# Early attention scores as float16 pairs, and one unit's keys and values kept, in a fused attention and two-layer kernel on Trainium2

## The chip, the cores and the metric

The kernel runs on one core of one Trainium2 chip. The metric is the device time of one launch in microseconds (us), as the median of several runs. A profile is one further execution, recorded by the hardware profiler; its time is given beside the runs.

## The reference

```python
scores = (1 / sqrt(D)) * q @ k.transpose(0, 1, 3, 2)       # B=2, H=8, S=768, D=64, float32
keep = (key < n_sink) | ((row - key >= 0) & (row - key < window))   # n_sink 4, window 128
a = softmax(where(keep, scores, -1e9))                     # sum + 1e-9
x = (a @ v) as a matrix of 1536 x 512
h = x @ moe_w_in;  x = (h * tanh(softplus(h))) @ moe_w_out          # 512 -> 2048 -> 512
h = x @ moe2_w_in; x = (h * clip(h + 3, 0, 6) / 6) @ moe2_w_out     # 512 -> 2048 -> 512
```

The four weight matrices arrive as float64. The attention's inputs and the output are float32.

## The kernel before

**Precision.** The dense layers work on float16 pairs: a float32 number, scaled by a power of two, becomes a high half (rounded by ScalarE) and a low half (the remainder, by VectorE's `scalar_tensor_tensor`). A product of two such numbers is three TensorE products: high by high, high by low, low by high. Weights are decoded to such pairs on the chip, one *weight tile* at a time (`gen_decode`, L201: one VectorE operation of L208, two of L209 and L210, ScalarE's high half at L213, VectorE's low half at L216).

**Units.** The 1536 rows are cut into 12 units of 128 rows, 6 for each of the two batches. A row sees the 128 keys of its own unit, the 128 of the unit before it (not for the first unit of a batch), and up to 16 first keys of the batch, the *sinks*. `BLOCKS` (L1009) puts the units in three blocks of four, `[[6,7,0,1],[2,3,4,5],[8,9,10,11]]`, which pass through the dense layers one after the other.

**Early units** are those of the first two blocks, in that order: 6, 7, 0, 1, 2, 3, 4, 5. The class `First` handles them in float32, half a unit (4 of the 8 heads) at a time:

- `load_first` (L235): three loads of 256 KB for keys, queries and values.
- `prep` (L263): TensorE transposes keys and queries (L271), ScalarE copies them out of PSUM in float32 as `kt1` and `qt` (L272).
- `scores` (L284): for each pair of heads, one float32 product per head and block of keys (L296; the profile records a float32 product twice). VectorE adds the mask and takes the row minimum (L300), ScalarE takes the exponential (L304).
- `turn` (L309): TensorE transposes the exponentials (L315); the copies `at` out of PSUM are ScalarE's (L317) or, for the second block of keys in a unit's first half, VectorE's (L319). The 16 sinks go the same way (L323 to L326).
- `values` (L328): products with the values (L334 and L341). `normalise` (L344): division by the sums, `xf` (L350). `outputs` (L352): transposes (L356), and a high half by ScalarE (L359) and a low half by VectorE (L360) into the dense layers' input `xt`.

`first_blocks` (L364) interleaves these steps: each half's scores stand ahead of the other half's products, and a unit is prepared a unit ahead. Weight tiles of the first layer are decoded beside them.

**Late units** 8 to 11 run as generators beside the first dense layer: `hook()` (L783), called between groups of dense products, takes pieces of them at rates set at the end of the file (`RATES`, `AHEAD`). `gen_front` (L446) and `gen_keys` (L426) convert keys, values and queries to float16 pairs and transpose keys and queries by DMA (L434, L460). Their scores are float16 products (L480), with row minima (L487). The exponentials become float16 pairs `ag` and are transposed by DMA (L511); `gen_back` (L548) multiplies them with the values (L557, L558, L568). Unit 8 needs the keys and values of unit 7 and the sinks of its batch: all three are loaded a second time and converted again for the late units (L418 to L424, L451 to L455, L516 to L525).

```python
        if u - 1 not in last:                                 # gen_front, L451
            if b not in ks:
                yield from gen_sinks(b)
            yield from gen_keys(u - 1)
            load_unit(u)
        yield from gen_keys(u)
```

**Order.** The Tile scheduler places the instructions on each engine's queue from the order of the code and their dependences. SyncE (SP) issues nearly all DMAs, in order. `watch` (L101) is a VectorE check of a 64-column piece for numbers too small for float16 pairs; such input would go to `general_path` (L852), which is not taken here.

Of the kernel before, what the change touches and what calls it, by code (L numbers as in the profile page):

```python
# [16 lines left out]
BIG = 1.0e30  # L17
# [12 lines left out]
def attention_moe_moe2(  # L30
# [201 lines left out]
    kv_n = {}  # L232
    sink_n = {}

    def load_first(u, names="kqv"):  # L235
# [8 lines left out]
    def first_sinks(b):  # L244


        ks1 = c_p.tile([128, HP, 16], F32, name=f"ks1_{b}")
        nc.scalar.activation(out=ks1, in_=kv_n[b * NSB][0][:, :, 0:16], func=AF.Copy)
# [6 lines left out]
        sink_n[b] = (ks1, vsb)  # L255

    class First:
# [5 lines left out]
        def prep(self):  # L263
            u, b, i = self.u, self.b, self.i
            kn, qn, vn = (qkv_n[u][nm] for nm in "kqv")
            kt1 = v_p.tile([128, HP, 144], F32, tag="k", name="kt1")
            self.qt = v_p.tile([128, HP, 128], F32, tag="q", name="qt1")
            for dst, src, sc in ((kt1[:, :, 0:128], kn, 1.0), (self.qt, qn, -1.0)):
                tp = ps_acc.tile([128, HP, 128], F32, tag="acc", name="tp")
                for h in range(HP):  # L270
                    nc.tensor.transpose(tp[:, h, :], src[:, 2 * h:2 * h + 2, :].rearrange("p a d -> p (a d)"), ident)  # L271
                nc.scalar.activation(out=dst, in_=tp, func=AF.Copy, scale=sc)  # L272
            kv_n[u] = (kt1, vn)
            if i == 0 and b * NSB + 2 in first:
                first_sinks(b)
            if i > 0 and b * NSB + 2 in first:
                nc.gpsimd.tensor_copy(out=kt1[:, :, 128:144], in_=sink_n[b][0])
            self.kvs = {0: [u], 1: [u - 1, u]}.get(i, [u, u - 1])
            self.kvs = [kv_n[x] for x in self.kvs]
            self.n = 128 * len(self.kvs) + (16 if i > 1 else 0)  # L280
            self.mask = (m0, m1, m2)[min(i, 2)]

        def scores(self, g):
# [5 lines left out]
            for h0 in (4 * g, 4 * g + 2):  # L289

                sps = [ps_h.tile([128, n], F32, tag="h", name="s") for _ in range(2)]
                for m, kv in enumerate(self.kvs):
                    w_ = n - 128 if m else 128
                    for r in range(2):
                        rows = slice(64 * r, 64 * r + 64)
                        nc.tensor.matmul(sps[r][:, m * 128:m * 128 + w_], self.qt[rows, h0 // 2, :], kv[0][rows, h0 // 2, 0:w_], start=True, stop=True)  # L296
                for r in range(2):
                    h = h0 + r
                    hh = h % 4
                    nc.vector.tensor_tensor_reduce(  # L300
                        out=d[:, hh, 0:n], in0=sps[r], in1=self.mask, scale=SCALE, scalar=BIG,
                        op0=ALU.add, op1=ALU.min, accum_out=self.mins[:, h:h + 1],
                    )
# [24 lines left out]
        def values(self, g):  # L328
# [3 lines left out]
            if self.i > 1:  # L332
                vsb = sink_n[self.b][1][:, g].rearrange("p h d -> p (h d)")
                nc.tensor.matmul(self.o[:, 4 * g:4 * g + 4, :], self.ats[g], vsb, start=fresh, stop=False, skip_group_check=True)  # L334
                fresh = False
# [64 lines left out]

    kt = {}
    vt = {}
    ks = {}
    vs = {}
# [13 lines left out]
    def load_late(u):  # L418
        if u is None:
            return  # L420
        if u - 1 in last:
            load_unit(u)
        else:
            load_unit(u - 1, "kv")  # L424

    def gen_keys(u):  # L426
# [13 lines left out]
        nc.vector.scalar_tensor_tensor(out=v16[:, 1], in0=vn, scalar=2.0 ** SV, in1=v16[:, 0], op0=ALU.mult, op1=ALU.subtract)  # L440
        if u == last[0] - 1:
            watch(k16[:, 0, 0, :])
            watch(v16[:, 0, 0, :])
        yield

    def gen_front(u):  # L446
        b, i = divmod(u, NSB)
        at_p, at1_p = late["at"], late["at1"]
        if u - 1 not in last:
            if b not in ks:  # L450
                yield from gen_sinks(b)  # L451
            yield from gen_keys(u - 1)
            load_unit(u)
        yield from gen_keys(u)
# [5 lines left out]
        nc.sync.dma_start_transpose(out=qt, in_=q16.rearrange("p t h d -> p (t h d)"))  # L460
        if u == last[0]:
            watch(q16[:, 0, 0, :])
        load_late(next_late(u))
# [52 lines left out]
    def gen_sinks(b):  # L516

        at1_p = late["at1"]
        ksn = at1_p.tile([128, 512], F32, tag="xf", name="ksn")[0:16].rearrange("p (h d) -> p h d", h=H)
        nc.sync.dma_start(out=ksn, in_=k[b, :, 0:16, :].rearrange("h p d -> p h d"))  # L520
        k16 = at1_p.tile([128, 2, DM], F16, tag="x16", name="k16s")[0:16].rearrange("p t (h d) -> p t h d", h=H)
        nc.scalar.activation(out=k16[:, 0], in_=ksn, func=AF.Copy, scale=2.0 ** SK)
        nc.vector.scalar_tensor_tensor(out=k16[:, 1], in0=ksn, scalar=2.0 ** SK, in1=k16[:, 0], op0=ALU.mult, op1=ALU.subtract)
        ks[b] = at1_p.tile([128, 2 * HP, 16], F16, name=f"ks_{b}")
        nc.sync.dma_start_transpose(out=ks[b], in_=k16.rearrange("p t h d -> p (t h d)"))  # L525
        yield
        vsn = at1_p.tile([128, 512], F32, tag="xf", name="vsn")[:, 0:2 * D].rearrange("p (g d) -> p g d", g=2)
# [519 lines left out]
```

## Time and profile before

| | before |
|---|---|
| runs | 625.07, 626.54, 623.51 us; median 625.07 |
| profiled execution: time, span | 623.05 us, 621.3 us |
| TensorE (PE) | 600.8 us, 97% of the span, 3400 instructions |
| TensorE weight load (PEld) | 307.6 us, 50% |
| VectorE (DVE) | 376.0 us, 61%, 688 instructions |
| ScalarE (ACT) | 354.6 us, 57%, 640 instructions |
| GpSimd (POOL) | 14.2 us, 2% |
| DMA | 72.10 MB, 116 GB/s |

Busy times overlap, so they don't add up to the span. Weight loads run beside products and are listed apart. A float32 product counts as two instructions. The granted TensorE clock is at its upper level (9 tenths or more) in all 40 slices of the page. The execution lasts 1.75 us longer than its span.

### The profile page before, as it was taken

Reading aid. Unit: us, or ns where it says so; the run is one execution under the profiler, and the core shown is the slowest. Engines: PE = TensorE matmul, PEld = TensorE weight load, DVE = VectorE, ACT = ScalarE, POOL = GpSimd, SP = SyncE. Lnnn points to the kernel's source line nnn. Section 1 sums busy time; section 2 is a strip of 40 time slices with the busy share of each in tenths; the row PEclk is TensorE's granted clock in tenths of the full one; section 3 lists DMA queues with packets and bytes.
Section 4 is the critical chain, followed back from the end, with each engine's and each line's share of the span. In section 5 each row is a group of like instructions: output and inputs, shape, how many; then the busy total and the mean of one; then the engine's idle time right before and its main releaser. Section 6 shows DMA issues by size and latency. Waiting matters only on the chain.

```text
span 621.3 us, 8731 instructions
## 1 busy us (share of the span) xinstructions
PE 600.8 (97%) x3400; PEld 307.6 (50%) x3400; DVE 376.0 (61%) x688; ACT 354.6 (57%) x640; POOL 14.2 (2%) x28
## 2 busy tenths in 40 slices
PE   8999999899989999899999999999999999999995
PEld 5888865444444445444444444444444444444442
DVE  5678787889988554626988999844432322422221
ACT  5887676887788676647686765453343331413131
POOL 0010000600000000000000000000000000000000
PEclk9999999999999999999999999999999999999999
DMA  9865146897479313100344434598800100100002
GB/s 188 195 130 170 69 143 150 218 244 210 135 205 205 55 37 54 37 18 0 136 136 136 148 124 152 193 333 304 304 0 1 44 25 0 69 1 0 1 0 73
DMA packets 105832, 72.10 MB, mean 116 GB/s; under 512 B 73512, under 2 KB 98088, under 8 KB 105784
## 3 DMA queue, kind: packets, MB, share of 16 engines
q1 hardware_dynamic: 105784, 71.48, 41.3%
q8 instruction: 28, 0.46, 0.3%
q14 instruction: 20, 0.16, 0.1%
HBM read 60.43 MB, written 3.15 MB: 102 GB/s over the span
## 4 chain that ended last, share of the span: by engine, by line
PE 68%; DVE 14%; ACT 9%; DMA 4%; issue 3%; SPq 1%; ACTq 0%; DVEq 0%
PE acc L725 27%; PE h L666 9%; PE h L668 9%; PE h L667 9%; PE o L341 4%; PE s L296 3%; DVE g L690 2%; DVE e L683 2%; PE tp L315 2%; DVE p L209 2%; DVE p L210 2%; ACT w L213 1%; ACT e L678 1%; ACT e L679 1%; DVE w L216 1%
## 5 line engine op out<-in xcount | busy, mean ns | idle before, releaser
L666 PE MATMUL h<-xt,w 128*128 128x512 f16 x384 | 145.6, 379 | 1.3 <-DVE e L683 1.3
L667 PE MATMUL h<-xt,w 128*128 128x512 f16 x384 | 145.5, 379 | 0.0
L668 PE MATMUL h<-xt,w 128*128 128x512 f16 x384 | 145.5, 379 | 0.0
L725 PE MATMUL acc<-g,w 128*128 128x512 f16 x576 | 129.5, 379 | 2.7 <-DVE g L690 2.2
L725 PE MATMUL acc<-w,g 128*128 128x512 f16 x576 | 128.1, 379 | 0.0
L685 DVE SCALAR_TENSOR_TENSOR e<-e,h 128x512 f32<-128x512 f32 x48 | 32.8, 686 | 97.8 <-ACT e L672 97.8
L725 PEld LDWEIGHTS <-g 128*128 128x128 f16 x576 | 56.3, 98 | 68.0
L725 PEld LDWEIGHTS <-w 128*128 128x128 f16 x576 | 55.4, 98 | 69.0 <-issue 3.8
L672 ACT ACTIVATE e<-h,bias 128x512 f32<-128x512 f32 x48 | 32.7, 683 | 95.7 <-PE h L668 95.7
L690 DVE SCALAR_TENSOR_TENSOR g<-e,g 128x1024 f16<-128x1024 f32 x48 | 58.7, 1223 | 25.1 <-ACT g L689 24.9
L689 ACT ACTIVATE g<-e 128x1024 f16<-128x1024 f32 x48 | 50.6, 1055 | 31.7 <-DVE e L685 17.9
L668 PEld LDWEIGHTS <-w 128*128 128x128 f16 x384 | 37.6, 98 | 45.2
L667 PEld LDWEIGHTS <-w 128*128 128x128 f16 x384 | 37.6, 98 | 44.7 <-issue 1.3
L666 PEld LDWEIGHTS <-w 128*128 128x128 f16 x384 | 37.6, 98 | 44.6
L216 DVE SCALAR_TENSOR_TENSOR w<-p,w 128x1024 f16<-128x1024 f32 x32 | 39.1, 1222 | 14.5 <-ACT w L213 14.5
L213 ACT ACTIVATE w<-p 128x1024 f16<-128x1024 f32 x32 | 33.7, 1053 | 21.5 <-DVE p L210 21.1
L670 ACT ACTIVATE e<-h 128x512 f32<-128x512 f32 x48 | 28.3, 589 | 25.6 <-PE h L668 25.3
L186 ACT ACTIVATE y<-y 128x512 int32<-128x512 int32 x32 | 20.0, 625 | 37.0 <-DVE y L184 36.9
L683 DVE SCALAR_TENSOR_TENSOR e<-e,h 128x512 f32<-128x512 f32 x48 | 30.7, 681 | 16.9 <-ACT e L680 16.9
L209 DVE SCALAR_TENSOR_TENSOR p<-raw,p 128x1024 int32<-128x1024 int32 x32 | 39.1, 1223 | 0.7
L210 DVE SCALAR_TENSOR_TENSOR p<-raw,p 128x1024 int32<-128x1024 int32 x32 | 39.1, 1222 | 0.3
L304 ACT ACTIVATE d<-d,mins 128x272 f32<-128x272 f32 (+2 forms) x64 | 30.4, 479 | 6.6 <-DVE mins L300 6.6
(141 smaller groups left out, 582.6 us busy)
## 6 DMA issues: line engine op xcount, KB each, us to landing
raw<-in_moe_w_in_dram SPq DMA_DIRECT2D x48, 512.0 KB, 3.9
raw<-in_moe_w_out_dram SPq DMA_DIRECT2D x48, 512.0 KB, 5.1
first<-in_k_dram SPq DMA_DIRECT2D x8, 256.0 KB, 5.2
first<-in_q_dram SPq DMA_DIRECT2D x8, 256.0 KB, 5.0
first<-in_v_dram SPq DMA_DIRECT2D x8, 256.0 KB, 5.2
out_dram<-part SPq DMA_DIRECT2D x8, 256.0 KB, 2.2
nk<-in_k_dram SPq DMA_DIRECT2D x5, 256.0 KB, 3.2
nv<-in_v_dram SPq DMA_DIRECT2D x5, 256.0 KB, 4.2
```

The source lines that it names most:

```text
L209: nc.vector.scalar_tensor_tensor(out=p, in0=lo_w, scalar=29, in1=p, op0=ALU.logical_shift_right, op1=ALU.bitwise_or)
L210: nc.vector.scalar_tensor_tensor(out=p, in0=hi_w, scalar=-0x40000000, in1=p, op0=ALU.bitwise_and, op1=ALU.bitwise_or)
L213: nc.scalar.activation(out=w[:, :, 0, :], in_=pf, func=AF.Copy, scale=2.0 ** SW)
L216: nc.vector.scalar_tensor_tensor(out=w[:, :, 1, :], in0=pf, scalar=2.0 ** SW, in1=w[:, :, 0, :], op0=ALU.mult, op1=ALU.subtract)
L666: nc.tensor.matmul(o, wh, x[:, 0, c, :], start=c == 0, stop=False)
L667: nc.tensor.matmul(o, wh, x[:, 1, c, :], start=False, stop=False)
L668: nc.tensor.matmul(o, wl, x[:, 0, c, :], start=False, stop=c == KD - 1)
L683: nc.vector.scalar_tensor_tensor(out=e[:, i], in0=e[:, i], scalar=2.5, in1=hps[i], op0=ALU.subtract, op1=ALU.mult)
L685: nc.vector.scalar_tensor_tensor(out=e[:, i], in0=e[:, i], scalar=6.0, in1=hps[i], op0=ALU.min, op1=ALU.mult)
L689: nc.scalar.activation(out=gh, in_=e, func=AF.Copy, scale=sc)
L690: nc.vector.scalar_tensor_tensor(out=gl, in0=e, scalar=sc, in1=gh, op0=ALU.mult, op1=ALU.subtract)
L725: nc.tensor.matmul(o, l_, r_, start=first and m == 0 and x == 0, stop=last and end and x == 2, skip_group_check=True)
```

## The change

- The early units' keys and queries leave PSUM as float16 pairs: the high half by ScalarE, a new low half by VectorE, for keys and for queries of each unit. Their scores are three float16 products in place of one float32 product.
- The copies `at` in `turn` are all ScalarE's; six of them were VectorE's.
- Unit 7's transposed keys (`kt_front`) and its values as a float16 pair (`v_front`) stay in SBUF. The late units read these in place of a second load, conversion and transpose.
- The sinks' keys (`ks`) are copied by GpSimd from the transposed keys of a batch's first unit; their late load, conversion and transpose go.
- q, k and v of unit 8 are loaded at once (`load_late`), and the late stream's first unit is taken in 4 pieces ahead of its place, not 7; the others stay at 3.
- The checks `watch` sit on unit 6's `kt1` and `qt` and on unit 7's values.

```diff
     class First:
...
-            kt1 = v_p.tile([128, HP, 144], F32, tag="k", name="kt1")
-            self.qt = v_p.tile([128, HP, 128], F32, tag="q", name="qt1")
-            for dst, src, sc in ((kt1[:, :, 0:128], kn, 1.0), (self.qt, qn, -1.0)):
+            if u == last[0] - 1:
+                kt1 = const.tile([128, 2 * HP, 144], F16, name="kt_front")
+            else:
+                kt1 = v_p.tile([128, 2 * HP, 144], F16, tag="k", name="kt1")
+            self.qt = v_p.tile([128, 2 * HP, 128], F16, tag="q", name="qt1")
+            for dst, src, sc in ((kt1[:, :, 0:128], kn, 2.0 ** SK), (self.qt, qn, -(2.0 ** SQ))):
                 tp = ps_acc.tile([128, HP, 128], F32, tag="acc", name="tp")
...
-                nc.scalar.activation(out=dst, in_=tp, func=AF.Copy, scale=sc)
+                nc.scalar.activation(out=dst[:, 0:HP], in_=tp, func=AF.Copy, scale=sc)
+                nc.vector.scalar_tensor_tensor(out=dst[:, HP:2 * HP], in0=tp, scalar=sc, in1=dst[:, 0:HP], op0=ALU.mult, op1=ALU.subtract)
...
+            if u == last[0] - 1:
+                kt[u] = kt1
+                vt[u] = v16 = const.tile([128, 2, H, D], F16, name="v_front")
+                nc.scalar.activation(out=v16[:, 0], in_=vn, func=AF.Copy, scale=2.0 ** SV)
+                nc.vector.scalar_tensor_tensor(out=v16[:, 1], in0=vn, scalar=2.0 ** SV, in1=v16[:, 0], op0=ALU.mult, op1=ALU.subtract)
+                watch(v16[:, 0, 0, :])
+            if i == 0:
+                ks[b] = const.tile([128, 2 * HP, 16], F16, name=f"ks_{b}")
+                nc.gpsimd.tensor_copy(out=ks[b], in_=kt1[:, :, 0:16])
...
+                    for tq, tk in ((0, 0), (0, 1), (1, 0)):
+                        for r in range(2):
+                            rows = slice(64 * r, 64 * r + 64)
+                            nc.tensor.matmul(
+                                sps[r][:, m * 128:m * 128 + w_], self.qt[rows, tq * HP + h0 // 2, :], kv[0][rows, tk * HP + h0 // 2, 0:w_],
+                                start=tq + tk == 0, stop=tq == 1,
+                            )
...
-                if m <= g:
-                    nc.scalar.activation(out=at[:, m], in_=tp, func=AF.Copy)
-                else:
-                    nc.vector.tensor_copy(out=at[:, m], in_=tp)
+                nc.scalar.activation(out=at[:, m], in_=tp, func=AF.Copy)
...
     def gen_front(u):
...
-        if u - 1 not in last:
-            if b not in ks:
-                yield from gen_sinks(b)
-            yield from gen_keys(u - 1)
-            load_unit(u)
+        if b not in vs:
+            yield from gen_sinks(b)
         yield from gen_keys(u)
...
-        ahead = {u: 3 if u - 1 in last else 5 if u // NSB in {x // NSB for x in last[:n]} else 7 for n, u in enumerate(last)}
+        ahead = {u: 3 if u // NSB in {x // NSB for x in last[:n]} else 4 for n, u in enumerate(last)}
```

Three places show how the instructions move. The first is ScalarE at the start, where units 6 and 7 are prepared and unit 6's first exponentials follow. Before:

```order
L272 ACTIVATE kt_207<-tp 128x4x128
L272 ACTIVATE qt_208<-tp 128x512
L272 ACTIVATE kt_221<-tp 128x4x128
L272 ACTIVATE qt_222<-tp 128x512
L304 ACTIVATE d,sums<-d,mins 128x128 x8
L317 ACTIVATE at<-tp 128x512
```

and now:

```order
L277 ACTIVATE kt_207<-tp 128x4x128
L277 ACTIVATE qt_208<-tp 128x512
L277 ACTIVATE kt_front<-tp 128x4x128
L277 ACTIVATE qt_230<-tp 128x512
L287 ACTIVATE v_front<-first 128x512
L327 ACTIVATE d,sums<-d,mins 128x128 x8
L339 ACTIVATE at<-tp 128x512
```

The conversion of unit 7's values, which needs their load (`first`), stands ahead of the eight exponentials.

The second place is SP's queue where the late units' loads begin (`nk`, `nv`, `nq` are keys, values and queries of a late unit, `raw` halves of weight tiles, `ksn` and `vsn` the sinks). Before, from the second load on, the first being unit 7's `nk`:

```order
L411 DMA nv<-in_v_dram 128x8x64
L520 DMA ksn<-in_k_dram 16x8x64
L411 DMA nq<-in_q_dram 128x8x64
L434 DMA_TRANSPOSE kt_1397<-k_1394 128x8x128
L411 DMA nk<-in_k_dram 128x8x64
L525 DMA_TRANSPOSE ks_1336<-k16s 128x8x16
L530 DMA vsn<-in_v_dram 64x1x64 x4
L166 DMA raw<-in_moe_w_in_dram 128x4x256
L170 DMA raw<-in_moe_w_out_dram 128x1024
L411 DMA nv<-in_v_dram 128x8x64
L434 DMA_TRANSPOSE kt_1439<-k_1436 128x8x128
L460 DMA_TRANSPOSE qt<-q_1486 128x8x128
```

and now:

```order
L166 DMA raw<-in_moe_w_in_dram 128x4x256
L428 DMA nq<-in_q_dram 128x8x64
L428 DMA nk<-in_k_dram 128x8x64
L428 DMA nv<-in_v_dram 128x8x64
L527 DMA vsn<-in_v_dram 64x1x64 x4
L447 DMA_TRANSPOSE kt_1628<-k_1625 128x8x128
L170 DMA raw<-in_moe_w_out_dram 128x1024
L467 DMA_TRANSPOSE qt<-q_1673 128x8x128
```

The first key transpose and the sinks' transpose are gone, and the second half of a weight tile (L170) stands behind a key transpose that waits for unit 8's converted keys.

The third place is TensorE at the values of the last late unit, unit 11, which need the transposed weights `atg`. Before:

```order
L668 LDWEIGHTS w
L668 MATMUL h<-xt_89,w 128x512
L666 LDWEIGHTS w
L666 MATMUL h<-xt_89,w 128x512
L557 LDWEIGHTS atg
L557 MATMUL o<-vs_1_1368,atg 128x256
L558 LDWEIGHTS atg
L558 MATMUL o<-vs_1_1369,atg 128x256
```

and now:

```order
L722 LDWEIGHTS w
L722 MATMUL acc<-g_3098,w 128x512
L554 LDWEIGHTS atg
L554 MATMUL o<-vs_1_1594,atg 128x256
L555 LDWEIGHTS atg
L555 MATMUL o<-vs_1_1595,atg 128x256
```

Before, 55 products of the dense layer stand between this unit's last scores and its values; now 66.

## Rows read from the trace of the kernel before

**Rows 1.** Busy by stretch: us, PE, PEld, DVE, ACT, POOL (count), PEclk, DMA, GB/s

```profile
20.00:80.00 60.00, 59.71 (x517) 50.93 (x516) 47.19 (x161) 45.03 (x134) 2.75 (x6) 1.00 0.52 138
98.70:200.00 101.30, 96.38 (x583) 45.13 (x584) 90.23 (x146) 80.05 (x133) 10.05 (x12) 1.00 0.81 193
365.00:613.00 248.00, 248.00 (x1150) 112.40 (x1149) 102.50 (x128) 86.85 (x149) 0.00 (x0) 1.00 0.26 90
```

**Rows 2.** TensorE's waits, 100 to 275 us: total us, times, longest

```profile
PE s L480 <- DMA qt<-q: 1.8, 1, 1.8
PE s L480 <- DVE mins L487: 1.6, 2, 1.4
PE o L557 <- DMA atg<-ag: 1.6, 1, 1.6
PE h L666 <- DVE e L683: 1.3, 1, 1.3
```

**Rows 3.** Timeline of an early half unit: start us, us, instruction, [idle before <- releaser]

```profile
56.55 0.51 ACT L304 ACTIVATE d<-d,mins 128x272 f32<-128x272 f32 x1
...
57.47 1.05 PE L315 MATMUL tp<-ident,d 128*128 128x128 f32 x8
...
58.35 0.27 PE L325 MATMUL tp<-ident,ds 128*64 128x128 f32 x1
...
58.56 1.21 PE L296 MATMUL s<-kt,qt 64*128 64x128 f32 x16
...
59.70 0.66 PE L356 MATMUL tp<-ident,xf 128*128 128x128 f32 x4
```

**Rows 4.** The same view, TensorE at float16 scores of a late unit

```profile
119.34 0.53 PE L480 MATMUL s<-kt,qt 64*128 64x128 f16 x12 [1.80 <-DMA qt<-q]
119.80 0.39 PE L666 MATMUL h<-xt,w 128*128 128x512 f16 x1
```

**Rows 5.** VectorE's groups to 98.7 us: busy us, mean ns, idle before

```profile
L360 DVE TENSOR_TENSOR xt<-tp,xt 128x512 f16<-128x512 f32 x7 | 4.8, 687 | 0.7 <-ACT xt L359 0.7
...
L208 DVE TENSOR_SCALAR p<-raw 128x1024 int32<-128x1024 int32 x6 | 4.1, 690 | 0.0
L209 DVE SCALAR_TENSOR_TENSOR p<-raw,p 128x1024 int32<-128x1024 int32 x6 | 7.3, 1224 | 0.1
```

**Rows 6.** The same view from 98.7 to 275 us

```profile
L440 DVE SCALAR_TENSOR_TENSOR v<-nv,v 128x512 f16<-128x512 f32 x5 | 3.5, 703 | 0.1
```

**Rows 7.** Timeline of the start, SP's queue and ScalarE

```profile
4.98 2.33 SPq L241 DMA_DIRECT2D first<-in_v_dram  x2
...
10.47 0.40 ACT L304 ACTIVATE d<-d,mins 128x128 f32<-128x128 f32 x1 [0.15 <-DVE mins L300]
```

**Rows 8.** DMA issues: count, KB each, median us from issue to landing

```profile
first<-in_v_dram SPq DMA_DIRECT2D x8, 256.0 KB, 5.2
...
nk<-in_k_dram SPq DMA_DIRECT2D x5, 256.0 KB, 3.2
...
qt<-q SPq DMA_TRANSPOSE x4, 4.9
```

**Rows 9.** Timeline from the last early unit to the first late scores

```profile
98.01 0.69 DVE L350 TENSOR_TENSOR xf<-o,ri 128x512 f32<-128x512 f32 x1 [3.16 <-PE o L341]
...
112.28 3.63 SPq L434 DMA_TRANSPOSE kt<-k  x1
...
115.97 1.29 SPq L460 DMA_TRANSPOSE qt<-q  x1
```

**Rows 10.** Timeline of the last late unit, SP's queue and TensorE

```profile
248.47 0.53 PE L480 MATMUL s<-kt,qt 64*128 64x128 f16 x12
...
259.02 2.21 SPq L511 DMA_TRANSPOSE atg<-ag  x1
...
263.47 0.28 PE L557 MATMUL o<-vs,atg 128*128 128x256 f16 x1 [1.58 <-DMA atg<-ag]
```

**Rows 11.** Weight loads of late scores, 119 to 275 us, columns as in rows 5

```profile
L480 PEld LDWEIGHTS <-qt 64*128 64x128 f16 x192 | 5.9, 94 | 10.6 <-issue 10.6
```

More of the change, by code (lines that the diff above doesn't have):

```diff
@@ L233, in attention_moe_moe2 @@
     sink_n = {}
+    kt = {}
+    vt = {}
+    ks = {}
     def load_first(u, names="kqv"):
@@ L244, in first_sinks @@
     def first_sinks(b):
-        ks1 = c_p.tile([128, HP, 16], F32, name=f"ks1_{b}")
-        nc.scalar.activation(out=ks1, in_=kv_n[b * NSB][0][:, :, 0:16], func=AF.Copy)
         vsn = c_p.tile([64, 2, D], F32, name=f"vsn_{b}")
@@ L254, in first_sinks @@
             nc.gpsimd.tensor_scalar(out=vsb[:, :, h, :], in0=vsn, scalar1=selh[0:64, h:h + 1], scalar2=None, op0=ALU.mult)
-        sink_n[b] = (ks1, vsb)
+        sink_n[b] = vsb
     class First:
@@ L271, in prep @@
                     nc.tensor.transpose(tp[:, h, :], src[:, 2 * h:2 * h + 2, :].rearrange("p a d -> p (a d)"), ident)
-                nc.scalar.activation(out=dst, in_=tp, func=AF.Copy, scale=sc)
+                nc.scalar.activation(out=dst[:, 0:HP], in_=tp, func=AF.Copy, scale=sc)
+                nc.vector.scalar_tensor_tensor(out=dst[:, HP:2 * HP], in0=tp, scalar=sc, in1=dst[:, 0:HP], op0=ALU.mult, op1=ALU.subtract)
             kv_n[u] = (kt1, vn)
[L274 to L277, printed above, removed]
+            if u == first[0]:
+                watch(kt1[:, 0, 0:64])
+                watch(self.qt[:, 0, 0:64])
+            if u == last[0] - 1:
[7 more added lines that the diff above has]
+                nc.gpsimd.tensor_copy(out=ks[b], in_=kt1[:, :, 0:16])
+                if b * NSB + 2 in first:
+                    first_sinks(b)
+            else:
+                nc.gpsimd.tensor_copy(out=kt1[:, :, 128:144], in_=ks[b])
             self.kvs = {0: [u], 1: [u - 1, u]}.get(i, [u, u - 1])
@@ L293, in scores @@
                     w_ = n - 128 if m else 128
-                    for r in range(2):
-                        rows = slice(64 * r, 64 * r + 64)
-                        nc.tensor.matmul(sps[r][:, m * 128:m * 128 + w_], self.qt[rows, h0 // 2, :], kv[0][rows, h0 // 2, 0:w_], start=True, stop=True)
+                    for tq, tk in ((0, 0), (0, 1), (1, 0)):
[5 more added lines that the diff above has]
+                            )
                 for r in range(2):
@@ L300, in scores @@
                     nc.vector.tensor_tensor_reduce(
-                        out=d[:, hh, 0:n], in0=sps[r], in1=self.mask, scale=SCALE, scalar=BIG,
+                        out=d[:, hh, 0:n], in0=sps[r], in1=self.mask, scale=SCALE * 2.0 ** -(SQ + SK), scalar=BIG,
                         op0=ALU.add, op1=ALU.min, accum_out=self.mins[:, h:h + 1],
@@ L332, in values @@
             if self.i > 1:
-                vsb = sink_n[self.b][1][:, g].rearrange("p h d -> p (h d)")
+                vsb = sink_n[self.b][:, g].rearrange("p h d -> p (h d)")
                 nc.tensor.matmul(self.o[:, 4 * g:4 * g + 4, :], self.ats[g], vsb, start=fresh, stop=False, skip_group_check=True)
@@ L399, in open_late @@
         late["kv"] = main.enter_context(tc.tile_pool(name="kv", bufs=3))
-    kt = {}
-    vt = {}
-    ks = {}
     vs = {}
@@ L418, in load_late @@
     def load_late(u):
-        if u is None:
-            return
-        if u - 1 in last:
+        if u is not None:
             load_unit(u)
-        else:
-            load_unit(u - 1, "kv")
     def gen_keys(u):
@@ L440, in gen_keys @@
         nc.vector.scalar_tensor_tensor(out=v16[:, 1], in0=vn, scalar=2.0 ** SV, in1=v16[:, 0], op0=ALU.mult, op1=ALU.subtract)
-        if u == last[0] - 1:
-            watch(k16[:, 0, 0, :])
-            watch(v16[:, 0, 0, :])
         yield
@@ L460, in gen_front @@
         nc.sync.dma_start_transpose(out=qt, in_=q16.rearrange("p t h d -> p (t h d)"))
-        if u == last[0]:
-            watch(q16[:, 0, 0, :])
         load_late(next_late(u))
@@ L518, in gen_sinks @@
         at1_p = late["at1"]
[L519 to L526, printed above, removed]
         vsn = at1_p.tile([128, 512], F32, tag="xf", name="vsn")[:, 0:2 * D].rearrange("p (g d) -> p g d", g=2)
```

## The prediction

> **What bounds the kernel now.** I read the table by stretches first. From 365 to 613 us TensorE is busy for 248.0 of 248 us, all of it products of the two dense layers [rows 1]. The change touches none of these, so whatever it gains or loses must arise before 365 us. From 20 to 80 us, where seven of the eight early units run, TensorE is busy for 59.7 of 60 us, VectorE for 47.2 [rows 1]: TensorE sets the pace, and VectorE has about 2 us of 10 left. From 98.7 to 200 us the dense layer runs with the late units beside it; VectorE is busy for 90.2 of 101.3 us there [rows 1], and TensorE's waits come into view. The waits of TensorE between 100 and 275 us are four kinds, 6.3 us in all: 1.8 for the first transposed late query, 1.6 for the row minima of late scores, 1.6 for the last transposed weights of attention, 1.3 for VectorE's product that frees a score bank [rows 2].
>
> Within an early unit the timeline shows a loop of half units: the last exponential of a half starts at 56.55 and ends at 57.06, and the transposes of that half start at 57.47 [rows 3]. Between a half's scores and its transposes TensorE works on the other half and on the unit before. So the loop through VectorE and ScalarE is short of the bound by only 0.4 us: a faster TensorE soon meets it.
>
> **The change part by part.**
> *Scores of the early units.* Today the eight float32 products of a half unit (sixteen records) start at 58.56, and the next work starts at 59.70: 1.14 us [rows 3]. The new form is the late units': twelve float16 products (two heads, two blocks of keys) start at 119.34 and the next work at 119.80: 0.46 us [rows 4]. A half unit needs 24 of them. Twice 0.46 less one change of the array's shape is 0.83; that change costs 0.10, since transposes step 0.88/8 = 0.11 apart while the step from the last one to the scores is 0.21 [rows 3]. The gain is 0.31 us in each of 12 half units with two blocks of keys, 3.7 us, and I estimate half of that, 0.15, in the 4 with one block: **-4.3 us**. The order mixes scores and 128-row work more finely: TensorE changes shape 64 times up to the end of the early units, not 56: 8 x 0.10 = **+0.7**. Bounds for the two together: -4.3 and 0 (the loop above takes TensorE's place).
>
> [...]
>
> *Low halves.* Each early unit adds two VectorE operations of 128x512 out of PSUM, as the one that makes the low half of its output does today: 0.69 us [rows 5]; 16 x 0.69 = 11.0. Six copies of the same shape leave VectorE for ScalarE, at 0.69 each by the same row, and unit 7's values add 0.70 (as L440, [rows 6]). VectorE gets 7.6 us more before the early units end. The order also puts a seventh weight tile there, where six stand today: 0.69 + 3 x 1.22 = 4.4 us [rows 5]. If two thirds of these 12.0 fall between 20 and 80 us, VectorE goes from 47.2 to 55.2 of some 57, or 97%. Work in VectorE's queue then stands ahead of minima for which exponentials, transposes and TensorE wait. The trace shows no such load. From below the cost is 0 (it fills idle time); from above it is one more 0.69 in each of 14 half-unit loops, 9.7 us. I take **+1.0**, near the lower end: the low halves are made a unit ahead of their scores, and what is pulled forward of the weight tile can wait.
>
> *The start.* Unit 7's values are now converted early: the order puts this copy on ScalarE ahead of the first exponential. Two loads of values are issued from 4.98 to 7.31, the second from about 6.15 [rows 7]; with 5.2 us from issue to landing [rows 8] it lands at 11.3, and a copy of at most 0.7 ends at 12.0. The first exponential starts at 10.47 today [rows 7]. That moves ScalarE's exponentials by 1.5. VectorE's low half of the same tile (0.70, [rows 6]) and its check, which I take at 0.4 like the 128-column exponential [rows 7], stand between the second and third minima: they end at 13.1, the third minimum at 13.4, while the third exponential could start at 12.9 or so. TensorE has little else to do then. 1.5 and 0.4 make **+1.9**; bounds 0 (the load lands sooner) and 2.6 (all of it in a row).
>
> *First late scores.* Unit 7's keys stay in SBUF: one load, one conversion and one transposing DMA fall away from the chain, and q, k and v of unit 8 are loaded at once. Today that unit's query transpose is issued at 115.97, behind a key transpose that holds SP's queue for 3.63 [rows 9]. In the new order the scores stand 12 products of the dense layer earlier on TensorE, some 11.9 us after the last normalisation, which today starts at 98.01 [rows 9]. The loads start with that normalisation: 3.2 to 4 to land, 3 more until VectorE, which has four other operations first, has the keys' low half, 1.4 and 0.5 of issues on SP, then 4.9 for the transpose [rows 8]: 12.3 to 14 us. The wait of 1.8 becomes 0.4 to 2.1: **-0.7**, bounds -1.8 and +1.5. One half of a weight tile now queues behind the key transpose on SP; VectorE can wait up to 3 us for it, ahead of the first late minima.
>
> *Late VectorE work.* 0.70 + 0.70 of unit 7 [rows 6] and the tile done earlier, 4.4, leave the stretch that is 89% busy. I take half of the 2.9 us that TensorE waits there for VectorE (1.6 + 1.3): **-1.5**, bounds -2.9 and +3 (that half tile).
>
> *The last late unit.* Today its last scores start at 248.47, the transpose of its converted weights is issued at 259.02, and the product that needs them starts at 263.47 after 1.6 us of waiting [rows 10]: TensorE wants them 13.4 us after the scores. With three steps less to run in the late stream, the new order puts 66 dense products there, not 55, that is 11 x 0.216 (248.0/1150, [rows 1]) = 2.4 us more, less 0.5 of late work that moves too: **-1.5**, bounds -1.6 and 0. Nothing is late next: the products that read this unit's output come 54 dense products later in the new order.
>
> Loads, GpSimd copies and the dropped conversions of the first keys of the batch cost nothing in the sum: two loads of 256 KB fewer, on a stretch where GpSimd is nearly idle. If the queues are fuller than I think, they are part of the bounds above.
>
> Sum: -4.3 + 0.7 + 1.0 + 1.9 - 0.7 - 1.5 - 1.5 = -4.4 us on the profiled 623.05, or 618.65. The median of the three runs is 625.07, 2.02 above; on that scale I forecast **620.7 us**.
>
> **Rivals.**
> 1. *The half-unit loop sets the pace.* TensorE gains nothing from faster scores, since transposes wait for exponentials. For: only 0.4 us lie between the last exponential's end and the transposes. Against: TensorE has no idle time there that shows such a wait now. The -4.3 falls away: -0.1, or 625.0.
> 2. *VectorE becomes the bound of the early units, and the kernel is slower.* For: 97% by the count above, and one queue for minima, low halves and weight tiles. Against: low halves are wanted late. Price: 9.7 in place of 1.0, and no gain of 4.3: +8.6, or 633.7. It decides once VectorE's idle time between 20 and 80 us falls from 13 us to about 2.
> 3. *Everything falls into place.* No cost on VectorE (-1.0), all of the 2.9 us (-1.4), all of the query wait (-1.1): -7.9, or 617.2, and 614.6 if the start is hidden (-1.9) and the added shape changes cost nothing (-0.7); I round the range's end down to 614.
> 4. *Float16 weight loads don't overlap.* 336 loads of 94 ns [rows 11] are 31.6 us against today's 12 x 1.14 and half as much for the other 4, 16.0: +15.6 in place of -4.3, or 640.6. Against: 192 such loads are busy for only 5.9 us together, which the products overlap. [...]
>
> That the change might not do what it says is excluded by the order: late scores read the kept keys, and late products the kept values.
>
> **How the numbers follow.** A change under 0.5%, 3.1 us, cannot be told from none: faster is below 621.9, slower above 628.2. My forecast gets 0.50, with a range of its own from 617.5 to 624; it lies 1.2 below the border, so I count 0.39 of it faster and 0.11 the same. Rival 3 gets 0.13 (faster), rival 1 0.23 (same), rival 2 0.11 and rival 4 0.03 (both slower). Faster 0.52, same 0.34, slower 0.14. From 614 to 628 all but the two slower rivals is held, with the bounds of the start and the query wait.
>
> **What would show it.** Right: groups of 24 float16 products in about 0.8 us; the first early exponential at about 12 us; the last normalisation of the early units 1 us earlier than 98.0 to level with it; the wait for the transposed weights near 261 us gone; the stretch from 365 us on unchanged. Wrong: VectorE above 95% from 20 to 80 us with TensorE waiting for minima (rival 2), transposes that wait for exponentials in every half unit (rival 1), a first exponential still near 10.5, or a new wait over 2 us at the first late scores.

## The result and the profile after

The changed kernel takes 627.31 us (median of 20 runs, 625.53 to 636.15) against 624.5 (median of 20, 623.31 to 627.5): ratio 1.0062, interval 1.0044 to 1.0081. It is slower by 0.6%, where 620.7 was forecast. The ratios here and below, and the clocks in the table of runs, leave out runs more than 1.5% above the fastest of their kernel: one of the changed kernel (636.15 us), one of e14 (904.57 us) and four of the kernel before. The profiled execution of the changed kernel took 632.77 us, one of its longer ones: its mean clock is 0.979, and 15 of the 20 runs had 0.985 or more. So its length is not compared with the median.

The page of the changed kernel, its first lines and the row of the granted clock (40 slices of the span):

```profile
span 631.0 us, 8957 instructions
...
PE 606.9 (96%) x3512; PEld 310.3 (49%) x3512; DVE 381.1 (60%) x696; ACT 358.1 (57%) x643; POOL 14.8 (2%) x30
...
PEclk9599998999999999999999999999999999999999
```

The second slice reads 5 and the seventh 8, where the kernel before has 9 in all slices. The table by stretches of the changed kernel shows it closer (columns as in [rows 1]):

```profile
10.00:13.00 3.00, 1.18 (x13) 0.66 (x9) 2.46 (x14) 1.68 (x6) 0.00 (x0) 1.00 1.34 218
13.00:34.00 21.00, 21.00 (x144) 17.54 (x143) 12.25 (x51) 13.34 (x46) 1.06 (x4) 0.52 0.70 172
38.00:98.00 60.00, 59.26 (x586) 46.16 (x585) 53.15 (x155) 48.23 (x127) 3.44 (x6) 1.00 0.51 135
105.00:110.00 5.00, 4.22 (x16) 2.10 (x16) 4.93 (x7) 1.73 (x4) 1.26 (x2) 0.66 0.90 233
365.00:613.00 248.00, 247.28 (x1147) 111.99 (x1146) 109.23 (x135) 91.94 (x152) 0.00 (x0) 1.00 0.28 98
```

The same stretches of the kernel before:

```profile
10.00:13.00 3.00, 2.84 (x24) 2.11 (x24) 1.81 (x16) 2.85 (x14) 0.00 (x0) 1.00 1.33 218
13.00:34.00 21.00, 20.78 (x184) 17.73 (x183) 14.00 (x59) 17.48 (x59) 1.71 (x5) 1.00 0.86 206
```

From 10 to 13 us TensorE is now busy for 1.18 us, not 2.84. Then its granted clock is 0.52 for 21 us, that is, at its lower level (0.50 in every whole microsecond from 14 to 34 us) nearly throughout; it is back at 1.00 after 34 us. TensorE is busy for all of those 21 us and yet issues 144 instructions where 184 were issued. A second fall lies between 105 and 110 us. The stretch from 365 us on is nearly as before [rows 1].

The timeline of the changed kernel's start shows why TensorE has nothing to do:

```profile
10.34 0.68 DVE L278 SCALAR_TENSOR_TENSOR qt<-tp,qt 128x512 f16<-128x512 f32 x1
10.95 0.28 DVE L323 CUSTOM_DVE_ANT_0 d<-s,m 128x128 f32<-128x128 f32 x1
...
11.29 0.54 PE L316 MATMUL s<-kt,qt 64*128 64x128 f16 x6 [1.20 <-DVE mins L323]
11.32 0.63 ACT L287 ACTIVATE v_front<-first 128x512 f16<-128x512 f32 x1 [1.03 <-DMA first<-in_v_dram]
11.86 0.39 ACT L327 ACTIVATE d<-d,mins 128x128 f32<-128x128 f32 x1
11.98 0.69 DVE L288 SCALAR_TENSOR_TENSOR v_front<-first,v_front 128x512 f16<-128x512 f32 x1 [0.54 <-ACT v_front L287]
...
12.39 0.71 PE L338 MATMUL tp<-ident,d 128*128 128x128 f32 x2 [0.56 <-ACT d L327]
...
12.73 0.28 DVE L323 CUSTOM_DVE_ANT_0 d<-s,m 128x128 f32<-128x128 f32 x1
```

Low halves stand ahead of the first minimum (10.95), ScalarE waits for unit 7's values and converts them (11.32) ahead of the first exponential (11.86, [rows 7] have 10.47), and their low half stands ahead of the third minimum (12.73).

TensorE's waits between 100 and 275 us answer to [rows 2]; those of the dense layer and the late units are:

```profile
PE h L663 <- DVE e L680: 3.6, 2, 2.2
PE o L554 <- DMA atg<-ag: 1.7, 1, 1.7
PE s L485 <- DVE mins L492: 1.1, 1, 1.1
...
PE s L485 <- DVE e L680: 0.3, 1, 0.3
PE s L485 <- DMA qt<-q: 0.2, 1, 0.2
```

The wait for the query transpose nearly went (1.8 to 0.2), but that for VectorE's e (a tile of the dense layer's activation) grew from 1.3 to 3.6, and that for the last transposed weights stayed.

In the profiled executions, the first normalisation comes at 25.58 us (19.32 before), the last at 105.21 (98.01, [rows 9]), and the span ends 9.7 us later: 6.3 us are lost before the first, 0.9 between the two, 2.5 behind the last. The lower clock reaches over the first of these marks, to 34 us, so the 0.9 holds some of its cost too.

### The profile page after: what moved, and what is told of

Its sections match the earlier page's. It is cut to its first block, busy times and chain, and to the rows that moved or that the text cites. A ratio compares the mean times of both kernels' runs of the same rounds, so it can differ in the third digit from the quotient of the medians.

```text
span 631.0 us, 8957 instructions
## 1 busy us (share of the span) xinstructions
PE 606.9 (96%) x3512; PEld 310.3 (49%) x3512; DVE 381.1 (60%) x696; ACT 358.1 (57%) x643; POOL 14.8 (2%) x30
## 4 chain that ended last, share of the span: by engine, by line
PE 67%; DVE 15%; ACT 10%; issue 3%; DMA 2%; SPq 1%; ACTq 0%; DVEq 0%
PE acc L722 28%; PE h L663 9%; PE h L665 9%; PE h L664 9%; PE o L361 4%; DVE p L209 3%; DVE w L216 2%; DVE p L210 2%; PE tp L338 2%; PE s L316 2%; DVE g L687 2%; DVE p L208 2%; DVE e L680 2%; ACT w L213 2%; ACT e L675 1%
## 5 line engine op out<-in xcount | busy, mean ns | idle before, releaser
L722 PE MATMUL acc<-g,w 128*128 128x512 f16 x576 | 131.3, 382 | 2.5 <-DVE g L687 2.0
L216 DVE SCALAR_TENSOR_TENSOR w<-p,w 128x1024 f16<-128x1024 f32 x32 | 39.1, 1222 | 11.9 <-ACT w L213 11.9
L184 DVE TENSOR_SCALAR y<-raw 128x1024 int16<-128x1024 int16 x32 | 22.1, 689 | 19.5 <-DMA raw<-in_moe_w_out_dram 19.3
```

The lines of the kernel that those rows point to most:

```text
L216: nc.vector.scalar_tensor_tensor(out=w[:, :, 1, :], in0=pf, scalar=2.0 ** SW, in1=w[:, :, 0, :], op0=ALU.mult, op1=ALU.subtract)
L722: nc.tensor.matmul(o, l_, r_, start=first and m == 0 and x == 0, stop=last and end and x == 2, skip_group_check=True)
```

## The experiments

All medians are set against the kernel before in the same job (624.2 to 624.7); the clock is the mean granted clock of each run, lowest to highest. Where rows of two jobs are compared below, half a microsecond is within the doubt. "Pace" means three empty pieces in the late stream (e8).

The profiled execution of the kernel before, whose rows the prediction used, had a mean clock of 0.998. Of the 99 others that the ratios keep, 86 had 0.995 or less. So that profile, with the clock at its upper level in every slice, was one of the better executions.

| run | edit | median us | ratio (interval) | clock |
|---|---|---|---|---|
| after | the change | 627.31 | 1.0062 (1.0044 to 1.0081) | 0.975 to 0.992 |
| e1 | values later | 625.64 | 1.0022 (1.0005 to 1.0038) | 0.984 to 0.991 |
| e2 | start filler | 624.38 | 1.0009 (0.9992 to 1.0026) | 0.987 to 0.995 |
| e3 | before, stalled | 632.9 | 1.0128 (1.0106 to 1.015) | 0.981 to 0.991 |
| e4 | kept unit 7 alone | 629.87 | 1.0081 (1.0062 to 1.0099) | 0.991 to 0.995 |
| e5 | scores alone | 627.99 | 1.0055 (1.0037 to 1.0072) | 0.982 to 0.986 |
| e6 | copies back | 628.23 | 1.0085 (1.0056 to 1.0115) | 0.973 to 0.989 |
| e7 | values later, filler, copies back | 629.44 | 1.0087 (1.0064 to 1.011) | 0.983 to 0.988 |
| e8 | filler, pace | 622.74 | 0.9959 (0.9943 to 0.9975) | 0.990 to 0.997 |
| e9 | two fillers | 626.85 | 1.0022 (1.0006 to 1.0037) | 0.993 to 0.997 |
| e10 | two fillers, pace | 622.71 | 0.9973 (0.9956 to 0.999) | 0.990 to 0.997 |
| e11 | pace | 624.81 | 1.0025 (0.9996 to 1.0053) | 0.977 to 0.991 |
| e12 | values later, filler, pace | 620.21 | 0.9923 (0.9904 to 0.9943) | 0.994 to 0.996 |
| e13 | values later, pace | 620.84 | 0.9937 (0.992 to 0.9954) | 0.991 to 0.994 |
| e14 | kept unit 7, pace | 625.83 | 1.0025 (1.0008 to 1.0042) | 0.980 to 0.996 |

### The start and the clock: e1, e2, e3

e1 moves the four lines on `v_front` from `prep` into a method that is called behind unit 7's normalisation, with a write that orders them:

```diff
+            nc.vector.tensor_scalar(out=v16[:, 0, 0, 0:H], in0=self.sums, scalar1=0.0, scalar2=None, op0=ALU.mult)
             nc.scalar.activation(out=v16[:, 0], in_=vn, func=AF.Copy, scale=2.0 ** SV)
```

e2 adds to the change, in `first_blocks`:

```diff
         us[0].scores(0)
+        br = ps_acc.tile([128, 512], F32, tag="acc", name="br")
+        for _ in range(10):
+            nc.tensor.matmul(br, us[1].qt[:, 0, :], us[1].qt[:, 0:4, :].rearrange("p a n -> p (a n)"), start=True, stop=True)
         us[0].scores(1)
```

e3 adds to the kernel before the conversion of unit 7's values in `prep` (kept in `stall`), and in `scores`:

```diff
+            if self.u == first[0] and g == 0:
+                nc.vector.tensor_copy(out=d[:, :, 0:4], in_=stall[0][:, 0, 0, 0:16].rearrange("p (h s) -> p h s", h=4))
```

> The changed kernel, with the conversion of unit 7's values made to wait until unit 7's own row sums are known (a 128x8 VectorE write into the tile, from those sums, orders it); nothing else differs. Theory (the clock): the conversion at the start leaves TensorE with little work from 10 to 13 us, and the granted clock then falls to 0.50 from 13.2 to 34 us of the profiled run. Without it the first exponential starts at about 11.3, not 11.86, the mean clock returns to about 0.998, and the time to 620 to 621 us. Rival (VectorE): the low halves fill VectorE in the early units; moving one of them changes nothing, 626 to 628 us at a clock that stays near 0.99. Third possibility: the four low halves of units 6 and 7 alone, 2.7 us on VectorE, leave TensorE idle long enough; then the clock still falls, 624 to 627 us.

> The changed kernel, with ten more products of 128x512 float16 (2.2 us) between the first scores of unit 6, into a bank that nobody reads: they only keep TensorE at work from 10.3 us. All of VectorE's and ScalarE's work stands where the change put it. Theory (the clock): no fall of the granted clock after 13 us, 620 to 622 us in spite of added work. Rival (VectorE bound, or the late stream): the added products cost 0 to 2 us, 627 to 629 us.

> The kernel before, with unit 7's values converted at the start for nobody, and a 128x16 copy of them into the first exponentials' tile, so that unit 6's first row minima wait for the conversion; scores stay float32, no low halves. Theory (the clock): TensorE starves from about 10.5 to 12.5 us, the clock falls as in the changed kernel, and the time rises by the 2 us of the stall and 5 to 10 us of slow clock: 630 to 637 us, mean clock 0.975 to 0.99. Rival: the stall alone, 626 to 627 us at 0.998.

Stretches of e2, then of e1, then of e3:

```profile
10.00:13.00 3.00, 2.64 (x18) 0.96 (x18) 2.52 (x14) 1.72 (x6) 0.00 (x0) 1.00 1.35 218
13.00:34.00 21.00, 20.42 (x229) 17.13 (x228) 17.16 (x74) 19.27 (x67) 1.69 (x5) 1.00 0.83 203
```

```profile
10.00:13.00 3.00, 1.78 (x18) 1.01 (x13) 2.46 (x17) 1.99 (x10) 0.00 (x0) 0.71 1.32 216
13.00:34.00 21.00, 20.87 (x206) 17.47 (x206) 14.74 (x65) 17.16 (x60) 1.06 (x4) 0.88 0.75 187
```

```profile
10.00:13.00 3.00, 0.31 (x6) 0.12 (x4) 0.85 (x3) 0.93 (x2) 0.00 (x0) 0.82 1.36 217
13.00:34.00 21.00, 20.73 (x151) 18.38 (x152) 12.46 (x60) 16.18 (x59) 3.92 (x7) 0.78 0.71 174
```

With ten useless products in the gap (e2) TensorE is busy for 2.64 of the 3 us, the clock stays at 1.00, and the median is 2.9 us lower than the change's although work was added. With the values later (e1) TensorE still has a gap of 1.2 us ahead of the second half of the scores, and the clock still falls to 0.50, for a shorter time in this execution (11.2 to 18 us). And in the kernel before, a stall of that kind alone (e3; its longest wait is 3.0 us) brings the fall, to 0.50 from 12 to 22 us, and costs 8.7 us, with the stall itself and two more falls further on in it. So the fall of the clock behind a gap in TensorE's work is shown, in both kernels.

The profiles of all runs agree. The seven in which TensorE waits over 1 us for the first minima (3.0 us in e3, 1.2 in the change, e1, e5, e6, e11 and e13) have a clock of 0.50 somewhere between 10 and 20 us. The three without that wait (before, e4, e14; 0.2 us) and the six with fillers (e2, e7 to e10, e12) have 1.00 throughout there. How long such a fall lasts differs by execution: 21 us in the profile of the change, 6.8 us (12.6 to 19.4) in that of e11, whose start is the same.

The expected 620 to 621 us of e1 and 620 to 622 us of e2 didn't come: the clock was not all. The time of e1 lies in the range of its third possibility, that the low halves alone leave TensorE idle long enough.

### The halves, and what follows the early units: e4, e5, e6, e7, e9

e4 is the change with float32 scores, copies and sinks as before; behind unit 7's normalisation it converts the sinks' keys, unit 7's keys and its values:

```diff
+                nc.scalar.activation(out=hi, in_=src, func=AF.Copy, scale=sc)
+                nc.vector.scalar_tensor_tensor(out=lo, in0=src, scalar=sc, in1=hi, op0=ALU.mult, op1=ALU.subtract)
```

e5 is the kernel before with `prep`, `scores` and `first_sinks` of the change (no values converted, no `watch` in `prep`). e6 takes one line of the change back, and e7 is e1 with that and with eight fillers as in e2:

```diff
-                nc.scalar.activation(out=at[:, m], in_=tp, func=AF.Copy)
+                if m <= g:
+                    nc.scalar.activation(out=at[:, m], in_=tp, func=AF.Copy)
+                else:
+                    nc.vector.tensor_copy(out=at[:, m], in_=tp)
```

e9 adds to e2, in the last early unit:

```diff
+            if f is None:
...
+                for _ in range(NF):
+                    nc.tensor.matmul(br, xs[:, 0, :], xs, start=True, stop=True)
             e.values(1)
...
+NF = 6
```

> The kernel before with only the second half of the change: unit 7's keys and values and the sinks' keys are kept as float16 pairs for the late units (converted from the float32 tiles once unit 7's row sums are known), the late stream is shortened as in the change. Early scores stay float32, the copies stay where they were. Theory (only the start and the clock went wrong): the late terms of the prediction come, up to 3.7 us less three added operations, 621 to 623 us. Rival (the late terms are wrong: VectorE's and the transposes' waits only move): 624 to 626 us, and the waits of TensorE between 100 and 275 us still sum to 6 us or more.

> The kernel before with only the first half: early queries and keys as float16 pairs and their scores as float16 products; the late units load and convert unit 7 and the sinks as before, and the copies of transposed exponentials stay where they were. No values are converted at the start, but four low halves still stand ahead of the first minima. Theory (clock): the gap at the start is shorter (first minimum at about 10.7, not 12.7 for the third), so the clock falls for a shorter time or not at all; from the first output of unit 6 to the last normalisation 2.5 us less than before; 621 to 625 us with a clock of 0.988 to 0.995. Rival (VectorE bound): no gain between those two marks and waits of TensorE for minima, 625 to 628 us.

> The changed kernel with the six copies of transposed exponentials given back to VectorE, as before. Theory: the second fall of the clock (105.9 to 109 us in the changed kernel's profile, 97.8 to 100.9 with the filler) follows waits of TensorE for these copies on ScalarE (0.7 us) ahead of the last outputs; with them gone it does not fall there, 1.5 to 2 us less: 625 to 626 us, the start unchanged. Rival (it follows the wait for the last normalisation, which stays): 627 to 628 us.

> The changed kernel with three mends at once: unit 7's values converted later, eight filler products among unit 6's first scores, the six copies back on VectorE. Theory (clock): no fall of the clock before 200 us, mean clock 0.995 to 0.998, 621 to 622.5 us, faster than both kernels. Rival (the late stage takes back what the early units gain): 623.5 to 625 us at that clock.

> The kernel of e2 with six more filler products (1.3 us) ahead of the last early unit's second half of values, where TensorE waits for sinks' weights and for copies on ScalarE (0.4 and 0.7 us at 93 to 95.5). Theory (clock): the fall of the clock at 97.8 to 100.9 us goes, 1 to 2 us less than e2, 622.5 to 623.5 us, at a mean clock near 0.998. Rival (the fall follows the wait for the last normalisation, or comes at random): it stays, 624 to 625 us.

Each half alone is slower than before. In e5 the clock falls twice: it is 0.71 from 10 to 13 us and 0.88 from 13 to 34, and 0.57 from 95 to 107, where the last early unit waits 2.1 us for a copy on ScalarE. From its first to its last normalisation (22.50 to 100.75) it gains 0.4 us, not the expected 2.5. Its time lies in its rival's range, but not for the rival's reason: TensorE waits 0.2 us for minima between those marks. e4 was a miss on both sides (621 to 623 us expected, 624 to 626 by its rival). Its larger waits between 100 and 275 us sum to 8.7 us, as its rival had it (6 or more):

```profile
PE h L669 <- DVE e L686: 3.6, 2, 2.2
PE s L491 <- DMA qt<-q: 2.2, 1, 2.2
PE o L560 <- DMA atg<-ag: 1.8, 1, 1.8
PE s L491 <- DVE mins L498: 1.1, 1, 1.1
```

e6 and e7 were misses. In e6, with the copies back, the last early unit waits for a copy on ScalarE longer (2.1 us, 0.7 in the change), and the clock is at its lower level from 96.5 to 106.8 us. In e7 that wait is 0.7 again, but the clock is at its lower level from 97.7 to 104.5 us, and between 100 and 275 us TensorE waits 5.8 us for VectorE's e, more than in any other run. e9 (622.5 to 623.5 us expected) came out above its rival's range too. It moved a fall and did not remove it: the one at 97.8 us is gone, one at 112.6 us follows a wait of 2.0 us for the first late query. Filling single gaps by hand there led nowhere.

### The pace of the late stream: e8, e10, e11, e12, e13, e14

e8 adds these lines to e2; they make e10 of e9, e11 of the change, e13 of e1 and e14 of e4, and e12 is e13 with five fillers:

```diff
         if b not in vs:
+            for _ in range(3):
+                yield
             yield from gen_sinks(b)
...
-        ahead = {u: 3 if u // NSB in {x // NSB for x in last[:n]} else 4 for n, u in enumerate(last)}
+        ahead = {u: 3 if u // NSB in {x // NSB for x in last[:n]} else 7 for n, u in enumerate(last)}
```

> The kernel of e2 (change and start filler) with three empty pieces ahead of the late stream's first unit, and 7 in place of 4 taken ahead: the pieces that the change removed are counted again, so that late attention work stands at about the same places of the dense layer as before. Theory (pace): with three pieces fewer the late work comes earlier, bunches with weight decoding, and TensorE waits 3.6 us for VectorE's e where it waited 1.3; with the pieces back the waits between 100 and 275 us fall from 8.8 us (e2) to 5 to 6.5, and the time to 620.5 to 622.5 us. Rival (the late terms were never there): waits only move, 623.5 to 625 us.

> Both together: the three empty pieces and both fillers. Theory: 619 to 621.5 us, faster than both kernels, with a mean clock of 0.996 to 0.998. Rival (neither pace nor the second fall decides): 623 to 625 us.

> The changed kernel with only the three empty pieces (and 7 taken ahead), no filler at the start. Theory (two separate causes): the start's slow clock stays (0.50 for 7 to 21 us from about 12 us on), the late stage is as in e8; against the change, the late pace gives back about 1.6 us (e8 against e2), 625 to 627 us at a mean clock of 0.985 to 0.99. Rival (the pace is nearly all of it): 622 to 624 us.

> The kernel of e8 with unit 7's values converted later as well (as in e1) and five fillers at the start, not ten. Theory: the third minimum no longer stands behind a conversion, so the first output of unit 6 comes 1 us sooner than in e8 (20.0, not 20.96) and the clock holds at the start; if the late stage keeps e8's order, 621.5 to 622.5 us. Rival (the order of the late stage comes out otherwise, as in e7): 623.5 us or more, with new waits of TensorE between 95 and 200 us.

> The kernel of e12 without its five filler products: unit 7's values later and the three empty pieces. Theory (the clock at the start is a cause of its own): low halves and checks still stand ahead of the first minima, TensorE is short of work from 10 to 11.3 us, the clock falls near 11.5 us as in e1 (6.6 us at half there), and the time is 2 to 4 us above e12: 622 to 624 us at 0.988 to 0.991. Rival (with the third minimum free the filler does nothing): 620 to 621 us at 0.994 or more.

> The kernel of e4 (float32 scores, unit 7 kept) with the three empty pieces. Theory (pace): of e4's 5.2 us over the kernel before, the part behind the last normalisation (4.5 us) goes: 624.5 to 626.5 us, and its waits between 100 and 275 us fall from 9 us to 5 to 6.5. Rival (keeping unit 7 is itself what costs there): 628 us or more.

The empty pieces take no time of any engine; they only let `hook()` count what the change had removed. Each kernel gains by them: 1.6 us (e2 to e8), 2.5 (the change to e11), 4.1 (e9 to e10), 4.8 (e1 to e13), 4.0 (e4 to e14), by the medians. The profiles show where: from the last normalisation of the early units to the end of the span, the seven kernels that keep unit 7 without the pieces (the change, e1, e2, e4, e6, e7, e9) take 525.2 to 529.4 us, the six with them 520.9 to 524.2, and the kernel before 523.3. Four forecasts of times were off all the same: e8 and e10 came out above theirs, e12 below, e11 between its range and its rival's.

The waits of e8 between 100 and 275 us:

```profile
PE o L559 <- DMA atg<-ag: 1.6, 1, 1.6
PE h L668 <- DVE e L685: 1.4, 1, 1.4
PE acc L727 <- DVE g L692: 0.7, 1, 0.7
PE s L490 <- DVE mins L497: 0.4, 1, 0.4
PE h L668 <- DVE mins L497: 0.2, 1, 0.2
```

They sum to 4.3 us, against 7.8 in e2 (not 8.8, as the expectation has it), and those for e are at 1.4 again. What the pieces pull apart stands in the changed kernel's timeline just ahead of 200 us:

```profile
196.62 1.04 ACT L512 ACTIVATE ag<-d 128x1024 f16<-128x1024 f32 x1
...
197.56 1.04 ACT L677 ACTIVATE e<-e 128x1024 f32<-128x1024 f32 x1
197.69 1.23 DVE L515 SCALAR_TENSOR_TENSOR ag<-d,ag 128x1024 f16<-128x1024 f32 x1 [1.57 <-ACT ag L512]
...
198.83 1.28 DVE L680 SCALAR_TENSOR_TENSOR e<-e,h 128x512 f32<-128x512 f32 x2
199.57 0.38 PE L663 MATMUL h<-xt,w 128*128 128x512 f16 x1 [2.22 <-DVE e L680]
```

A conversion of a late unit's weights stands ahead of the dense layer's activation on both engines (1.04 us on ScalarE, 1.23 on VectorE), and TensorE waits 2.2 us for the bank. With the pieces back, the order turns: in e8 VectorE's e comes at 201.35 us and the low half of the weights behind it at 202.56.

e13 and e12 are faster than both kernels. Their difference, 0.6 us, lies within their intervals: with the values out of the way the filler decides nothing that these runs can tell, although the clock of e13 still falls behind its gap (0.92 from 13 to 34 us, a fall of 3.4 us). So e13 missed its forecast of 2 to 4 us above e12; the rival's time came, with a clock lower than the rival had. e13 against the change removes no work and adds one 128x8 operation: 627.31 to 620.84. The two edits are worth more together (6.5 us) than one by one (1.7 in e1, 2.5 in e11); why was not settled. e14 came as expected and stays 1.3 us above the kernel before, so keeping unit 7 alone gains nothing even at the old pace. The likely reason, not tested by itself, is that its conversions from float32 tiles are added work in the early units: the last normalisation came 2.4 us later in e4 (100.42 against 98.01).

## Why the prediction was wrong

**The start failed, in its price.** The step said "TensorE has little else to do then", took +1.9 and set the bounds at 0 and 2.6. The stall was about right: with the clock held (e2) the first normalisation comes 1.7 us later than before. But the clock fell behind the very stretch in which TensorE has little to do (busy for 1.18 of 3 us, then 0.52; with the filler of e2 2.64, then 1.00). Every row that I read had the clock at 1.00, so the sum had no term for it. In the profiled executions the change and e2 differ by 8.0 us at the last normalisation (105.21 and 97.24), but that fall was a long one; over the medians the filler is worth 2.9 us. With the pace set right it is worth 2.1 (e11 to e8), which fits a fall of 6.8 us as in e11: its first normalisation comes at 23.34 us, that of e8 at 20.96. In the profile of the change no wait of TensorE in the stretch from 10 to 13 us is over 1.2 us, and 21 us at 0.52 follow; none of the four rivals was about the clock.

**The scores were right, as far as their sum goes.** From the first to the last normalisation of the early units the sum had -4.3 + 0.7 + 1.0 = -2.6. The rows of e13 and of e2 with the clock at 1.00 for all or nearly all of that stretch:

```profile
21.30 0.69 DVE L374 TENSOR_TENSOR xf<-o,ri 128x512 f32<-128x512 f32 x1
...
96.37 0.69 DVE L374 TENSOR_TENSOR xf<-o,ri 128x512 f32<-128x512 f32 x1 [0.73 <-PE o L365]
```

```profile
21.02 0.69 DVE L370 TENSOR_TENSOR xf<-o,ri 128x512 f32<-128x512 f32 x1
...
97.24 0.69 DVE L370 TENSOR_TENSOR xf<-o,ri 128x512 f32<-128x512 f32 x1
```

That is 75.07 and 76.22 us, against 78.69 before (19.32 to 98.01): -3.6 and -2.5. The three terms were not measured one by one, but the first can be read. A half unit's float16 scores in the changed kernel:

```profile
55.79 0.82 PE L316 MATMUL s<-kt,qt 64*128 64x128 f16 x22
56.53 0.66 PE L376 MATMUL tp<-ident,xf 128*128 128x128 f32 x4
```

It is 0.74 us to the next work, for 22 of the 24 products; all 24 start at 55.72, 0.81 us ahead of it, where 0.83 was taken. Rivals 1 and 4 fall with it. Rival 2 falls too: from 38 to 98 us VectorE is busy for 53.2 of 60 us and TensorE for 59.3. The low halves cost about what was taken, or less.

**The late terms failed, -3.7 us in all.** The waits that they were about went from 6.3 to 6.9 us. "First late scores" looks right, since its wait went from 1.8 to 0.2, but part of that is likely luck: the clock was at its lower level from 105.8 to 109.2 us, so TensorE came to these scores later. In e9, with the clock at 1.00 up to there, the wait is 2.0 us, inside the step's 0.4 to 2.1 but no gain. (The step has these scores 12 products of the dense layer earlier. From the last normalisation on, 84 such products stand ahead of them before and 49 now; its 11.9 us goes with 49.) "Late VectorE work" counted what leaves VectorE, 2.9 us of waits to be halved; they became 5.0 (3.6 + 1.1 + 0.3), because the stream of late pieces, three pieces shorter at the same rate, ran its conversions into the dense layer's activations. "The last late unit" counted 11 products more between scores and values; but the conversion is paced by the same hooks. In the changed kernel:

```profile
253.36 0.53 PE L485 MATMUL s<-kt,qt 64*128 64x128 f16 x12
...
266.45 1.97 SPq L516 DMA_TRANSPOSE atg<-ag  x1
...
270.91 0.28 PE L554 MATMUL o<-vs,atg 128*128 128x256 f16 x1 [1.75 <-DMA atg<-ag]
```

The transpose is issued 13.1 us behind the scores, not 10.6 [rows 10], and the wait is 1.7. I had read the order of one engine and left the others where they were. With the pieces back and no fall of the clock between the last normalisation and 300 us, that part of the kernel is 1.7 us (e13) and 2.3 us (e11) shorter than before: some of the -3.7 was there, once the pace let it come.

**The sum.** With both failures undone and the rest of the change kept, e13 is 3.7 us below the kernel before, where -4.4 was forecast. Part of that agreement is luck: in e13 the wait for the last transposed weights is still 1.6 us, and the early units gain 1 us more than the sum had.

**Left open.** What each late fall of the clock (near 97, 105, 112, 136, 155 or 195 us, by kernel and execution) follows was not settled; e6 and e9 show only that it moves with the waits around the last early unit. In the profiled execution of e14 the clock is at its lower level from 29.9 to 47 us, and TensorE has no wait over 0.3 us between 20 us and then. So a fall can come without a gap that the profile shows.

## What to carry to other kernels

Price a gap in TensorE's work twice: by its length, and by what the products behind it take at the lower clock (here 0.52 for 21 us in one profile, 2.9 us over the medians of the change and e2); a profile whose clock is at its upper level in every slice doesn't show that price, and may be one of a kernel's better executions (here 0.998, where 86 of 99 others had 0.995 or less). Where side work is dealt out by a count of pieces, a change that removes pieces also moves every piece behind them: keep the count, or set the rates anew, before judging the change. And where an early load feeds an operation that nobody needs yet, tie that operation to something later, or a scheduler may put it ahead of the first work that matters.

## What the runs showed of the hardware

- In the profile of the changed kernel the granted clock fell to its lower level (0.50) behind gaps of which none was over 1.2 us, and stayed there for 21 us of TensorE fully busy (13 to 34 us, clock 0.52); such a fall lasted a shorter time in others (6.8 us in e11, 3.4 in e13). One fall, in e14 at 29.9 us, came with no wait of TensorE over 0.3 us since 20 us.
- One program, the changed kernel, ran between 0.973 and 0.992 of mean clock, and its time went along: 636.15 to 625.53 us.
- The kernel before ran between 0.989 and 0.998 over 99 executions; its profile had 0.998.
- Ten added products of 128x512 made the changed kernel faster by 2.9 us (627.31 to 624.38, medians).
